# The down-projection of a retention and SwiGLU kernel as seven block products a group, with a new order of work

## The chip, the cores and the metric

The kernel runs on one core of a Trainium2 chip. The core has a matrix engine (TensorE, "PE" in the profile; its weight loads are shown as "PEld"), a vector engine (DVE), a scalar engine (ACT), GpSimd (POOL), and a queue that issues transfers (SyncE, "SP"). POOL also issues transfers. Each engine works through its own instructions in program order and waits on semaphores for the others. The metric is the device time of one execution in microseconds, and less is better.

## The reference

Two layers follow each other. The first is a recurrent retention over 768 positions, for 4 batches and 8 heads of 64 numbers; the second is a feed-forward layer with a gate:

```python
for t in range(S):
    state = gamma * state + einsum('bhd,bhe->bhde', k[:, :, t], v[:, :, t])
    y[:, :, t] = scale * einsum('bhd,bhde->bhe', q[:, :, t], state)
x  = y transposed to (3072 tokens, 512)
xn = x / sqrt(mean(x * x) + 1e-6) * rms_g
g  = xn @ w_gate                      # 512 x 1536
out = (g * sigmoid(g) * (xn @ w_val)) @ w_out      # 1536 x 512, float32 out
```

The last product, hidden values times `w_out`, is the down-projection.

## The kernel before

The 768 positions are cut into six chunks of 128. A *group* c is chunk c of all four batches b, 512 tokens. The state is not updated position by position: within a chunk the outputs come from masked scores, and the state is added once a chunk.

A group passes through these steps, each an operation with a short name:

- `Lq`, `Lk`, `Lv` (L304-316) load q, k, v of one chunk. Issued by POOL they are cast to bf16 on the way; issued by SP they arrive in f32 and `Cq`, `Ck`, `V` (L333-358) scale or cast them. For group 0, POOL's q and k loads come in a packed form ("q8", "k8", L310-312), which needs another way of transposing. Loads of group 2 wait for the last piece of `w_out` (L315-316).
- `Tq`/`Tk` with `Eq`/`Ek` transpose q and k on TensorE and copy the result out (groups 0 and 1); `tq`/`tk` (L387) do it by a transfer on SP's queue (groups 2 to 5). The packed form takes 16 small matmuls with the matrix `pick` (L364-367), the plain form four with `ident` (L371). `J` (L506) transposes the packed k back.
- `A` (L395) makes the scores of one or two batches, `M0`, `M1` (L421) mask them on DVE, `Y` (L432) multiplies them with v and adds the part from the state. `P` (L407) is a form of A for batches 2 and 3 of group 4 that starts the state's part early.
- `S` (ACT), `R` (POOL), `N` (DVE) are the normalization, `X` with `XE`, or `XE` on SP alone, the transposing of its result to `xnT`.
- `K` (L521) makes a chunk's addition to the state, four matmuls of 128x128x128 for the pairs of heads, of which only the blocks on the diagonal are used; `U` (L530) adds it to `st_f` on DVE, and `B` (L537, POOL) copies the state to bf16 for the next chunk.
- `g` and `v` (`ffn`, L544) are the two products of the feed-forward layer, four matmuls of 512 columns for each of 12 hidden tiles; `s` (ACT) and `h` (DVE) make the hidden values `hT`.
- `d` (L570) is the down-projection: for each batch 12 matmuls of 512 columns, accumulated over the hidden tiles in one PSUM bank; `o` copies the bank to SBUF, `st` stores it. The very last batch is cut into three pieces of columns (`e`, L593).
- `wg`, `wv`, `wo` load pieces of the weights through POOL's queue. `H` and `hot` are matmuls without use that keep TensorE busy in the first microseconds while data is on its way.

The order of all this is a list written out by hand or by a planner ahead of time, the string `ORDER` (L17-100): `g.2.5.6.0.4/5` is the operation g for group 2, hidden tiles 5 to 6, batches 0 to 4, in PSUM bank 5, and `@D`, `@A`, `@P`, `@S` choose the engine (DVE, ACT, POOL, SP). The loop at L600-604 issues the operations in that order, so each engine's own order is the list's. The eight PSUM banks are shared: an operation that takes a bank waits until the one before has been read out.

Of the kernel before, what the change touches and what calls it, by code (L numbers as in the profile page):

```python
# [9 lines left out]
F32 = mybir.dt.float32  # L10
# [7 lines left out]
H.8/3 yt Lk.0.2@S ident Ck.0.2@D vd Lk.1.1@S iota Tk.0.2/0 rms.1@S D.0.2@D Lk.0.0@P Lq.0.1@P H.3/1 Tk.0.0/2  # L18
H.1/1 Tq.0.1/7 Ek.0.0@D mk1 hot.3/1 J.0.0/3 D.0.0@D mk0 Lq.0.0@P Lk.0.1@P Tq.0.0/6 Lq.0.2@P Eq.0.1@A Eq.0.0@A
Tk.0.1/5 Ek.0.1@A Ek.0.2@D yd Lk.0.3@P H.1/1 Tq.0.2/4 tab Lq.0.3@P Eq.0.2@D hot.2/0 A.0.0/5017 M0.0.0 G/2 M1.0.0  # L20
Tq.0.3/6 Lv.0.0@P M0.0.1 GE@A Tk.0.3/3 Eq.0.3@A Lv.0.1@P M1.0.1 Lv.0.2@P Lv.0.3@P wg.0.2 Y.0.0/4 wv.0.2 A.0.2/21
wg.2.4 M1.0.2 Ek.0.3@A Lq.1.1@P H.3/0 A.0.3/61 S.0.0 M0.0.2 H.1/0 Y.0.2/3 K.0.0/0 J.0.1/5 M1.0.3 R.0.0 S.0.2
N.0.0 M0.0.3 Y.0.1/1 H.1/2 X.0.0/4 J.0.3/7 wv.2.4 S.0.1 XE.0.0@D U.0.0@A R.0.2 R.0.1 Ck.1.1@A N.0.2 B.0.0 H.2/2
Y.0.3/0 g.0.0.2.0.1/2 K.0.2/6 S.0.3 s.0.0.2.0.1 N.0.1 U.0.2@A wg.4.6 X.0.2/4 R.0.3 XE.0.2@D D.0.1@D
v.0.0.2.0.1/3 X.0.1/2 wv.4.6 causal XE.0.1@A Lk.1.2@P v.0.0.2.2.3/4 wg.6.9 Lq.1.2@P wv.6.9 h.0.0.2.0.1
g.0.0.2.2.3/6 D.0.3@D Lq.1.0@P g.0.0.2.1.2/5 g.0.2.3.0.3/3 s.0.0.2.2.3 h.0.0.2.2.3 s.0.0.2.1.2 g.0.3.4.0.3/6
N.0.3 v.0.0.2.1.2/4 D.1.1@D Tq.1.1/5 Lk.1.0@P Tk.1.1/0 X.0.3/7 Eq.1.1@D K.0.1/2 wg.9.12 v.0.3.4.0.3/1 Lv.1.1@P
s.0.3.4.0.3 XE.0.3@A g.0.0.4.3.4/6 s.0.2.3.0.3 h.0.0.2.1.2 g.0.4.6.3.4/4 wv.9.12 g.0.4.5.0.3/7 v.0.4.6.3.4/5
v.0.2.3.0.3/3 U.0.1@D s.0.4.6.3.4 Ek.1.1@A h.0.3.4.0.3 g.0.5.6.0.3/0 s.0.4.5.0.3 h.0.4.6.3.4 mc.0@P mc.1@P
v.0.4.5.0.3/5 v.0.0.4.3.4/7 h.0.2.3.0.3 Tk.1.2/1 g.0.6.7.0.4/4 Ek.1.2@A Lv.1.2@P h.0.4.5.0.3 g.0.7.8.0.4/2  # L30
Lv.1.0@P wo.0.4 Tq.1.2/1 s.0.5.6.0.3 s.0.7.8.0.4 Eq.1.2@D B.0.1 g.0.8.9.0.4/3 A.1.2/51 v.0.5.6.0.3/0 M1.1.2
wo.4.8 wo.8.12 s.0.0.4.3.4 v.0.7.8.0.4/2 h.0.0.4.3.4 h.0.5.6.0.3 h.0.7.8.0.4 Lk.1.3@P D.1.2@P Lk.2.0@S
v.0.6.7.0.4/7 Tk.1.0/0 M0.1.2 Lk.2.3@S Tq.1.0/6 v.0.8.9.0.4/1 s.0.6.7.0.4 Ek.1.0@A Eq.1.0@D h.0.6.7.0.4
s.0.8.9.0.4 Lq.2.1@S A.1.0/6042 M0.1.1 M1.1.0 B.0.2 M1.1.1 g.0.11.12.0.4/3 g.0.9.10.0.4/5 g.0.10.11.0.4/4
s.0.11.12.0.4 K.1.1/3 Y.1.1/0 s.0.10.11.0.4 h.0.8.9.0.4 S.1.1 U.1.1@D M0.1.0 v.0.9.10.0.4/2 v.0.10.11.0.4/3
R.1.1 v.0.11.12.0.4/4 s.0.9.10.0.4 K.0.3/7 h.0.9.10.0.4 D.1.0@P U.0.3@A Y.1.2/2 S.1.2 h.0.10.11.0.4 Y.1.0/3
N.1.1 h.0.11.12.0.4 Lq.1.3@P S.1.0 B.0.3 Lq.2.0@S Lk.2.1@S K.1.0/7 X.1.1/5 R.1.2 K.1.2/1 U.1.2@D d.0.3.0.4/0
N.1.2 R.1.0 N.1.0 d.0.0.0.4/6 XE.1.1@D d.0.1.0.4/4 d.0.2.0.4/2 X.1.0/5 d.0.3.4.8 X.1.2/1 d.0.0.4.8 Lv.1.3@P
d.0.1.4.8 XE.1.2@D d.0.1.8.12 U.1.0@D XE.1.0@A B.1.1 g.1.0.1.0.3/7 Tk.1.3/5 g.1.1.2.0.3/3 d.0.3.8.12 Tq.1.3/1
o.0.1@D Eq.1.3@D d.0.0.8.12 s.1.1.2.0.3 Ek.1.3@A o.0.3@A A.1.3/13 M1.1.3 Ck.2.0@A M0.1.3 tk.2.0 v.1.1.2.0.3/0  # L40
d.0.2.4.8 o.0.0@A Y.1.3/3 h.1.1.2.0.3 v.1.0.1.0.3/6 Ck.2.3@D S.1.3 R.1.3 Cq.2.1@D g.1.3.4.0.3/1 v.1.2.3.0.3/4
# [36 lines left out]
v.3.11.12.0.4/7 h.3.11.12.0.4 K.4.1/4 Lv.5.1@S Y.4.2.2 S.4.1 Y.4.3.2 S.4.2 V.5.1@P d.3.1.0.10/6 tk.5.3 tk.5.2
N.4.0 R.4.1 tk.5.1 st.2.0@S d.3.1.10.12 S.4.3 tq.5.3 N.4.1 R.4.3 o.3.1@A R.4.2 d.3.0.0.10/1 B.4.3 N.4.3 Lq.5.1@S
# [24 lines left out]
def kernel(  # L104
# [11 lines left out]
    nc = tc.nc  # L116
# [31 lines left out]
    def flat(x):  # L148
        return x.rearrange("p h d -> p (h d)")
# [485 lines left out]
```

## Time and profile before

| | |
|---|---|
| median of 3 runs | 233.62 us (233.48 to 234.39) |
| span of the profiled execution | 233.6 us (the page has no other time for it) |
| PE busy | 227.6 us |
| DVE, ACT, POOL busy | 130.4, 96.1, 89.7 us |
| mean granted clock of TensorE | 0.993 |
| moved by transfers | 33.61 MB, of which 25.70 MB by the hardware queue |
| read from and written to HBM | 28.31 MB, 6.29 MB |

Times in the traces count from the first instruction of the span. "Busy" matmul time overlaps from one matmul to the next, so the spacing of matmuls in the chain or the timeline is a better price than their mean duration. A bracket behind a row tells how long the engine had been idle before it, and what ended that.

### The profile page before, as it was taken

The numbers are of one execution on the slowest core, as the hardware profiler recorded it, in microseconds if no ns is written. First come the engines' busy times: TensorE is split into PE (matmuls) and PEld (weight loads), VectorE is DVE, ScalarE is ACT, GpSimd is POOL, SyncE is SP. The second block draws the span as 40 slices with busy tenths as digits, with TensorE's granted clock in tenths as the row PEclk, the third lists the DMA queues.
The fourth block names the chain that finished last, engine by engine and source line by source line (L and its number), as shares of the span: only waits on it lengthen the run. The fifth ranks groups of instructions, "written<-read, shape, count | busy, mean of one in ns | idle before, by whom it ended". The sixth has DMA issues, their size and how long they took to land.

```text
span 233.6 us, 4637 instructions
## 1 busy us (share of the span) xinstructions
PE 227.6 (97%) x1771; PEld 120.8 (52%) x1771; DVE 130.4 (56%) x241; ACT 96.1 (41%) x231; POOL 89.7 (38%) x163
## 2 busy tenths in 40 slices
PE   8799999999999999999999999999999999999994
PEld 2458855645545655445554444554455444444444
DVE  6479639753662965628975239866367532323320
ACT  7658433514337231464731346553265332232202
POOL 8958998550544555030273741247003100000000
PEclk9979999999999999999999999999999999999999
DMA  7999999999798888999988899968511400020222
GB/s 126 147 180 123 127 179 184 205 145 215 133 206 214 171 194 140 262 218 221 235 173 146 179 221 206 198 149 142 148 61 27 112 0 0 3 90 9 83 89 93
DMA packets 105353, 33.61 MB, mean 144 GB/s; under 512 B 94449, under 2 KB 102385, under 8 KB 105330
## 3 DMA queue, kind: packets, MB, share of 16 engines
q1 hardware_dynamic: 81858, 25.70, 50.2%
q0 software_dynamic: 23472, 7.60, 30.1%
q8 instruction: 14, 0.23, 0.4%
q14 instruction: 9, 0.07, 0.1%
HBM read 28.31 MB, written 6.29 MB: 148 GB/s over the span
## 4 chain that ended last, share of the span: by engine, by line
PE 89%; DMA 4%; POOL 2%; ACT 2%; DVE 1%; issue 0%; SPq 0%; POOLq 0%; DVEq 0%; ACTq 0%
PE v_ps L549 27%; PE g_ps L549 27%; PE o_ps L574 21%; PE a_ps L403 3%; DMA kb<-in_k_dram 3%; PE y_ps L441 2%; PE kv_ps L526 2%; PE y_ps L445 2%; DMA out_dram<-o_sb 1%; PE o_ps L596 1%; PE hot_ps L240 1%; PE t_ps L366 1%; PE t_ps L371 1%; PE xt_ps L495 1%; ACT xsq L455 1%; ACT xsq L458 1%
## 5 line engine op out<-in xcount | busy, mean ns | idle before, releaser
L567 DVE TENSOR_TENSOR hT<-sg,v_ps 128x512 bf16<-128x512 bf16 (+2 forms) x76 | 48.7, 656 | 47.8 <-PE v_ps L549 34.8
L549 PE MATMUL v_ps<-xnT,wv_b 128*128 128x512 bf16 (+2 forms) x344 | 71.2, 345 | 0.1
L559 ACT ACTIVATE sg<-g_ps 128x512 bf16<-128x512 f32 (+2 forms) x76 | 42.1, 575 | 70.6 <-PE g_ps L549 68.1
L549 PE MATMUL g_ps<-xnT,wg_b 128*128 128x512 bf16 (+2 forms) x344 | 70.0, 344 | 0.0
L574 PE MATMUL o_ps<-wo_b,hT 128*128 128x512 bf16 x276 | 63.5, 379 | 0.0
L549 PEld LDWEIGHTS <-wg_b 128*128 128x128 bf16 x344 | 30.4, 98 | 29.3
L549 PEld LDWEIGHTS <-wv_b 128*128 128x128 bf16 x344 | 30.2, 98 | 28.9 <-DVE am L426 0.6
L574 PEld LDWEIGHTS <-hT 128*128 128x128 bf16 x276 | 26.3, 98 | 29.1
L468 POOL TENSOR_SCALAR ms<-ssq 128x1 f32<-128x1 f32 x24 | 4.6, 190 | 59.1 <-ACT xsq L458 58.4
L426 DVE TENSOR_TENSOR am<-a_ps,causal 128x512 bf16<-128x512 f32 x32 | 20.6, 685 | 7.8 <-PE a_ps L403 7.5
L339 POOL TENSOR_TENSOR qb<-qf,ydec 128x512 bf16<-128x512 f32 x13 | 14.0, 1074 | 25.2 <-DMA qf<-in_q_dram 24.9
L146 ACT COPY o_sb<-o_ps 128x512 f32<-128x512 f32 (+1 forms) x16 | 8.8, 552 | 29.7 <-PE o_ps L574 23.1
L458 ACT ACTIVATE xsq<-y_ps 128x512 f32<-128x512 f32 x22 | 13.2, 599 | 18.9 <-PE y_ps L445 13.7
L482 DVE SCALAR_TENSOR_TENSOR xn<-y_ps,rstd,g_bc 128x512 bf16<-128x512 f32 x22 | 16.3, 748 | 4.3 <-POOL rstd L470 3.0
L146 DVE COPY o_sb<-o_ps 128x512 f32<-128x512 f32 (+1 forms) x10 | 6.4, 648 | 18.1 <-PE o_ps L574 12.2
L541 POOL CAST st_b<-st_f 64x256 bf16<-64x256 f32 x40 | 15.9, 398 | 1.3
L470 POOL TENSOR_TENSOR rstd<-ms,mhalf 128x1 f32<-128x1 f32 x24 | 13.3, 552 | 2.0
L534 DVE TENSOR_TENSOR st_f<-st_f,kv_ps 128x512 f32<-128x512 f32 x16 | 10.8, 684 | 5.2 <-PE kv_ps L526 4.6
L356 ACT ACTIVATE vp<-vf,vdec 128x64 bf16<-128x64 f32 x48 | 12.2, 343 | 0.0
L426 DVE TENSOR_TENSOR am<-a_ps,mask 128x512 bf16<-128x512 f32 x16 | 10.4, 686 | 2.5 <-PE a_ps L403 2.3
L240 PE MATMUL hot_ps<-one 128*128 128x512 bf16 x20 | 8.5, 547 | 1.1 <-DVE one L153 1.1
L441 PEld LDWEIGHTS <-am 128*128 128x128 bf16 x176 | 7.8, 99 | 3.1 <-issue 0.3
(99 smaller groups left out, 174.8 us busy)
## 6 DMA issues: line engine op xcount, KB each, us to landing
out_dram<-o_sb SPq DMA_DIRECT2D x23, 256.0 KB, 2.4
kf<-in_k_dram SPq DMA_DIRECT2D x18, 256.0 KB, 3.8
qf<-in_q_dram SPq DMA_DIRECT2D x16, 256.0 KB, 3.9
vf<-in_v_dram SPq DMA_DIRECT2D x16, 256.0 KB, 3.9
wo_b<-in_moe_w_out_dram POOLq DMA_DIRECT2D x3, 512.0 KB, 12.2
qb<-in_q_dram POOLq DMA_DIRECT2D x8, 128.0 KB, 6.6
vp<-in_v_dram POOLq DMA_DIRECT2D x8, 128.0 KB, 6.5
kb<-in_k_dram POOLq DMA_DIRECT2D x6, 128.0 KB, 5.9
```

The lines of the kernel that those rows point to most:

```text
L146: (e.copy if e is ACT else e.tensor_copy)(out, in_)
L339: e.tensor_tensor(out=u["qb"], in0=u["qf"], in1=ydec[:, c, :, None].to_broadcast([128, H, D]), op=ALU.mult)
L426: DVE.tensor_tensor(out=u["am"][:, i], in0=u["a"][i], in1=m, op=ALU.mult)
L441: nc.tensor.matmul(y[:, h, :], u["am"][:, h % 2, h // 2, :], u["vp"][:, h, :], start=h == 0, stop=c == 0 and h == H - 1, skip_group_check= ...
L458: ACT.activation(xsq, flat(u["y"]), AF.Square, accum_out=u["ssq"])
L470: POOL.tensor_tensor(out=u["rstd"], in0=ms, in1=mhalf, op=ALU.pow)
L482: DVE.scalar_tensor_tensor(out=u["xn"], in0=flat(u["y"]), scalar=u["rstd"], in1=g_bc, op0=ALU.mult, op1=ALU.mult)
L541: POOL.tensor_copy(st_b[b][r, :, i * 64:i * 64 + 64], st_f[b][r, :, i * 64:i * 64 + 64])
L549: nc.tensor.matmul(p[:, (n - n0) * m:(n - n0 + 1) * m], W[w][0][:, s, n * 128:(n + 1) * 128], xnT[c][:, s, b0 * C:b1 * C], start=s == 0, s ...
L559: ACT.activation(sg[:, :cols], done["wg", c, n0, b0][:, :cols], AF.Silu)
L567: DVE.tensor_tensor(out=hT[c][:, n0:n1, b0 * C:b1 * C], in0=sg, in1=p, op=ALU.mult)
L574: nc.tensor.matmul(o_ps[c, b], hT[c][:, n, b * C:(b + 1) * C], wo_b[:, n, :], start=n == 0, stop=n == NFF - 1)
```

## The change

**The down-projection.** The operations `d`, `o`, `st` and `e` are no longer used. The hidden values of a group are cut in two halves of tokens (batches 0 and 1, batches 2 and 3) and, within each block r of four hidden tiles, in two halves of tiles; `w_out` is cut in two halves of rows in the same way and in two halves of columns. The four quarters of the output are put together from seven products instead of eight:

- four sums of weights, once: w1 to w4 (each 1536 elements a partition, bf16);
- for each group and each of its three blocks r four sums of hidden quarters, z1 to z4 (each 512 elements a partition, bf16), on DVE or POOL; z3 takes the place of the quarter that it is made from;
- the products a1, a6, a7, a4 (in one bank, one on top of the other), b2, and c5, c3 (in one bank). One product is 12 matmuls of 256 columns: 2 halves of 128 tokens, 3 blocks r, 2 tiles each;
- between them the copies q1, q6, q7 of the bank a to SBUF, and the results r1 = b2 + q1, r2 = c5 + q7, r3 = c5 + c3 + q6 on DVE, and r4, a copy of the whole of a. s1 to s4 store the four quarters, 256 KB each.

**The state products** `K` become eight matmuls a chunk, one for each head, 64 columns wide and written to 64 partitions; `st_f` has half as many elements and `U` with it.

**Memory.** The masks share their buffers with the weight sums, two early tiles share the output buffers, `kd` and the z sums share twelve buffers, `hT` is kept in blocks of four tiles.

**The order** is new throughout. All eight q and k loads of group 0 are now in the packed form; four loads of group 1 stand ahead of the first weights; there are 12 matmuls of the kind H, not 20; the products of group 0 come in the middle of group 1's feed-forward work and those of group 3 in group 4's and 5's; the stores of results are spread out, and one of group 0 comes at the end.

The diff, cut to its core:

```diff
 ORDER = """
...
+hot.2/0 hot.3/1 Lq.0.1@P rms.1@S H.3/2 Lk.0.1@P Lq.0.3@P iota G/3 Lk.0.3@P Lk.0.0@P H.1/4 H.1/5 ident Lq.0.0@P
+Lq.0.2@P pick mk1 Lk.0.2@P vd H.1/6 Lv.0.3@P Tq.0.1/7 GE@D yt Lv.0.1@P mk0 Lv.0.0@P H.2/1 H.1/0 Eq.0.1@D Tq.0.3/2
+Tk.0.1/4 Ek.0.1@D Eq.0.3@A Tk.0.3/3 Tk.0.0/5 causal Ek.0.3@D Lv.0.2@P Tq.0.0/6 J.0.1/7 D.0.1@D A.0.3/10 M0.0.3
+Ek.0.0@A J.0.0/2 D.0.0@D Eq.0.0@A A.0.0/4356 J.0.3/7 Lk.1.3@P Lk.1.2@P M1.0.3 Y.0.3/1 S.0.3 Lk.4.2@S Lk.1.1@S yd
+Lq.1.2@P Tk.0.2/2 Lq.1.3@P Ck.1.1@A Ek.0.2@A M1.0.0 M0.0.0 K.0.0/0 Tq.0.2/3 Eq.0.2@A U.0.0@A D.0.3@D wg.2.4 wg.0.2
...
+v.0.6.7.0.4/0 h.0.6.7.0.4 g.1.6.7.0.4/6 s.0.8.9.0.4 g.1.1.2.0.3/2 v.0.7.8.0.4/3 Ck.2.2@P Lv.2.0@S s.1.2.3.0.3
...
+v.1.7.8.0.4/5 h.1.7.8.0.4 a1.0.0.3/1 A.2.2/2743 q1.0@D M0.2.3 B.1.1 g.1.11.12.0.4/6 tq.2.0 Lk.3.2@S s.1.11.12.0.4
...
+s.3.10.11.0.4 Lq.5.1@S Cq.5.1@P P.4.2/125406 M1.4.3 g.3.2.3.0.4/3 g.3.5.6.0.4/7 s.3.5.6.0.4 M0.4.3 M1.4.2 M0.4.2
...
+a4.5.2.3.0 r4.5.0@D c3.5.2.3.1 c3.5.2.3.0 a4.4.0.3 s4.5.0@S r3.5.1 r3.5.0 s3.5.0@S s3.5.1@S r4.4@A s4.4@S
...
-        u["kv"] = bank(bk[0], [128, NHP, 128], F32, "kv_ps")
-        for hp in range(NHP):
-            nc.tensor.matmul(u["kv"][:, hp, :], flat(k)[:, hp * 128:(hp + 1) * 128],
-                             u["vp"][:, 2 * hp:2 * hp + 2, :], start=True, stop=True)
+        u["kv"] = bank(bk[0], [128, NHP, D], F32, "kv_ps")
+        for h in range(H):
+            nc.tensor.matmul(u["kv"][h % 2 * D:h % 2 * D + D, h // 2, :], k[:, h], u["vp"][:, h, :],
+                             start=True, stop=True)
...
+    def quarter(c, r, i, j):
+        return hT[c, r][:, (J0, J1)[j], (LO, HI)[i]]
...
+    def zsum(i, e, c, r, x, a, b, how):
+        if x is None:
+            x = sb.tile([128, 2, GT // 2], BF16, name="z", tag="kd", bufs=KD)
+        e.tensor_tensor(out=x, in0=a, in1=b, op=how)
+        done["z", i, c, r] = x
...
+    def product(x, i, bk, c, r0, r1, p=None):
+        first = i in (1, 2, 5) and r0 == 0
+        if first:
+            done[x, c] = bank(bk[0], [128, 2, HM], F32, x)
+        for q in (0, 1) if p is None else (p,):
+            for r in range(r0, r1):
+                for k in (0, 1):
+                    nc.tensor.matmul(done[x, c][:, q], left(i, c, r)[:, k, q * C:q * C + C], right(i)[:, r, k],
+                                     start=first and q == r == k == 0, stop=r == 2 and k == 1, skip_group_check=True)
...
+    def keep(i, e, c):
+        done["q", i, c] = ring([128, 2, HM], F32, "sn", SN)
+        copy(e, done["q", i, c], done["a", c])
...
+    QUARTER = {1: ("b", 1, 0, 0), 2: ("c", 7, 1, 1), 3: ("c", 6, 0, 1), 4: ("a", None, 1, 0)}
...
+            DVE.tensor_tensor(out=done["r", i, c][:, s], in0=done[x, c][:, s], in1=done["q", q, c][:, s], op=ALU.add)
```

259 lines of the change are left out of this document (149 added, 110 removed).

## The prediction

> **What bounds the kernel now.** I read the page's busy shares and slices first, then the chain of work that ended last, then the groups by form and the engines' timelines.
>
> ```profile
> span 233.6 us, 4637 instructions
> ...
> PE 227.6 (97%) x1771; PEld 120.8 (52%) x1771; DVE 130.4 (56%) x241; ACT 96.1 (41%) x231; POOL 89.7 (38%) x163
> ...
>
> DMA  7999999999798888999988899968511400020222
> ...
> PE 89%; DMA 4%; POOL 2%; ACT 2%; DVE 1%; issue 0%; SPq 0%; POOLq 0%; DVEq 0%; ACTq 0%
> ```
>
> TensorE is busy from end to end and 89% of the last chain; no other engine passes 56%. But the DMA line stands mostly at 8 or 9 for the first 29 slices (170 us): the transfers are nearly as full as TensorE. A gain on TensorE counts only if the inputs come earlier too. The end, from the chain in order of time:
>
> ```profile
> 220.04 7.77 PE o_ps L574 x36
> 227.81 2.66 PE o_ps L596 x36
> 230.47 0.02 issue
> 230.50 0.32 ACT o_sb L146
> ```
>
> The last matmul ends at 230.47; a copy and a store take the other 3.13 us. All sums below are against the profiled span of 233.6, which is also the median of the runs (233.62).
>
> **The change part by part.** *The down-projection.* The group row counts what goes:
>
> ```profile
> L574 PE MATMUL o_ps<-wo_b,hT 128*128 128x512 bf16 x276 | 63.5, 379 | 0.0
> ...
> L596 PEld LDWEIGHTS <-hT 128*128 128x128 bf16 x36 | 2.7, 98 | 0.2
> ```
>
> Mean durations overlap (379 ns), so the price is the spacing in the chain: 7.77/36 = 215.8 ns for 512 columns, 0.4215 ns a column. The 36 matmuls of L596 (24 of 192 columns, 12 of 128: 6144) take 2.66, 0.433 ns a column. Before: 276 x 0.2158 + 2.66 = 62.2 us. After: 6 groups x 7 products x 12 matmuls = 504 of 256 columns. That width is not in the trace; between 0.4215 and 0.433 ns a column it costs 107.9 to 110.8 ns. I take the middle, 109.3: 55.1 us. **Saved: 7.1 us** (6.4 to 7.8). The 216 extra weight loads are free as long as a 98 ns load hides under its neighbour's 109 ns; at L596 loads of 98 ns already hide under matmuls spaced 74 ns.
>
> The Trainium skill, "TensorE: Matmul & The Clock Gate", section "Back-to-back issue gap", speaks against this: it gives a sustained spacing of 131 ns at 512 columns and 81 at 128, so half a width would cost far more than half. An estimate from that page is 98 ns at 256 columns, 49 us after against 38 before, and the sum would come out slower; the chain's 215.8 ns contradicts its 512-column figure, which leaves it the small chance below.
>
> *State products* (K, 20 of them): four 128-column matmuls become eight of 64 columns on 64-row outputs. The same shape stands in the early transposes (L366). From TensorE's timeline:
>
> ```profile
> 1.11 3.60 PE L240 MATMUL hot_ps<-one 128*128 128x512 bf16 x8 [1.11 <-DVE one L153]
> ...
> 7.42 0.44 PE L366 MATMUL t_ps<-pick,qb 128*64 128x64 bf16 x16
> 7.80 0.34 PE L234 MATMUL hot_ps<-one 128*128 128x128 bf16 x3
> ...
> 41.34 0.39 PE L526 MATMUL kv_ps<-vp,kd 128*128 128x128 bf16 x4
> 41.56 0.40 PE L441 MATMUL y_ps<-vp,am 128*128 128x64 bf16 x8
> ```
>
> Sixteen take 0.38 us start to start, so eight take 0.19, against 0.22 now: 20 x 0.03 = **0.6 us saved**. Against that, b = 2 of group 0 now comes in the packed form too: one more re-transpose J (0.22, as four of 128 columns) and 0.38 instead of 0.22 for its T: **0.4 lost**. TensorE's net: 7.1 + 0.6 - 0.4 = 7.3 us.
>
> *Sums and copies.* 72 z (512 bf16 elements a partition; 44 on DVE, 28 on POOL), 4 w (three times that), 18 q copies, and additions in place of 18 of the 24 output copies. No row shows bf16 + bf16 from SBUF; the neighbours:
>
> ```profile
> L146 DVE CAST kb<-kf 128x512 bf16<-128x512 f32 x8 | 3.3, 418 | 0.0
> ...
> L517 DVE TENSOR_TENSOR kd<-kb,vdec 128x512 bf16<-128x512 bf16 x3 | 2.1, 686 | 0.3 <-ACT vdec L259 0.3
> ...
> L517 POOL TENSOR_TENSOR kd<-kb,vdec 128x512 bf16<-128x512 bf16 x2 | 2.1, 1035 | 0.1
> ...
> L146 ACT COPY o_sb<-o_ps 128x512 f32<-128x512 f32 x14 | 8.2, 586 | 28.0 <-PE o_ps L574 23.1 <-DMA out_dram<-o_sb 4.8
> ```
>
> A z on DVE lies between 0.42 and 0.69; I take 0.42, as both its inputs are 16 bits wide and kd has an f32 one. DVE then goes from 130 to about 163 us (z 18, w 2, additions and copies 19 more, other moved work 4, less the old copies and the halved state additions, 11); at 0.69, 177. POOL: 28 x 1.04 + two w of 3.1 = 35, less 3 moved away: about 122. ACT falls to 88. All stay under the span, so I cost them at nothing on the path: TensorE's g and v of other groups cover them. Locally it is tight. In the stretch of 20 us of matmul work that ends at the first product, DVE has 15 us to do at 0.42 and 19 at 0.69; only the second would hold up banks, by 1 or 2 us. A slowed z delays h and state copies queued behind it on DVE, and those hold PSUM banks.
>
> DVE and POOL also meet. Around 125 us:
>
> ```profile
> 125.31 0.68 DVE L358 TENSOR_TENSOR vp<-vf,vdec 128x512 bf16<-128x512 f32 x1
> ...
> 125.52 1.37 POOL L339 TENSOR_TENSOR qb<-qf,ydec 128x512 bf16<-128x512 f32 x1 [2.22 <-DMA qf<-in_q_dram]
> ...
> 129.75 1.04 POOL L339 TENSOR_TENSOR qb<-qf,ydec 128x512 bf16<-128x512 f32 x1 [2.85 <-DMA qf<-in_q_dram]
> ```
>
> The same POOL instruction took 1.37 beside a DVE one that reads two SBUF tensors and 1.04 alone; DVE paid nothing (0.68). So each z on DVE can delay POOL by up to 0.33 us: at most 44 x 0.33 = 15 us on an engine with 100 us to spare, but POOL's q scalings stand behind it. The Trainium skill, "GPSIMD Engine Reference", section "Key points", says that the two share their SBUF interfaces, with contention when DVE has two SBUF inputs; these rows agree.
>
> *The start.* POOL issues the loads and the weights in order:
>
> ```profile
> 6.17 3.59 POOL L314 DMA_DIRECT2D vp<-in_v_dram  x4
> ...
> 9.99 0.76 POOL L323 DMA_DIRECT2D wg_b<-in_moe_w_gate_dram  x1 [0.23 <-DMA kb<-in_k_dram]
> ...
> DMA to landing us min/median/max: 4.9/7.2/10.7
> ```
>
> The last row is wv_b's. Four group-1 loads (0.9 each) and one more group-0 load now stand ahead of the weights, so the first wg issue moves from 10.0 to about 15 and wv.4.6 to about 26.4, behind four R and both mc. First g: about 22.8 instead of 19.4, but by then all of group 0's and much of group 1's attention is done; the useful matmul work done by 22.8 is equal, 9.9 us. wv.4.6 lands at 31 to 34 (26.4 + 4.9 to 7.2); the old kernel has as much done by 31.3 as the new one at that point. So the start costs 0 to 2: **+1.0**. The fillers H drop from 20 to 12 (8 x 0.45, by the first row of the fence on TensorE, or x 0.22 at full clock: 1.7 to 3.6 us), but they only filled waits for data, so I count nothing; if data came no later, that would be gain. PEclk falls to 7 in the third slice even with them; a second such slice would cost 0.3 x 5.8 = 1.7 us, inside these bounds.
>
> *The middle.* Group 2's loads wait for the last piece of wo, and so does w1 on POOL, with group 2's q scalings (Cq) queued behind its 3.1 us:
>
> ```profile
> 50.77 1.01 SPq L314 DMA_DIRECT2D kf<-in_k_dram  x2
> ...
> 149.35 0.62 PE L403 MATMUL a_ps<-qT,kT 64*128 64x128 bf16 x16
> ...
> 165.58 0.55 PEld L549 LDWEIGHTS <-wv_b 128*128 128x128 bf16 x4 [0.61 <-DVE am L426]
> ...
> L387 SPq DMA_TRANSPOSE kT<-kb x16: 1195/1222/1681, 57.5 to 162.4; - x16
> ...
> L314 SPq DMA_DIRECT2D qf<-in_q_dram x16: 572/580/1457, 51.8 to 153.2; - x16
> ```
>
> wo should land about 0.7 later, at 51.5. w1 to 54.6, Cq's to 57.7, transposes behind them: the first scores of group 2 can start at about 66.5, and TensorE comes to them at about 68. Then the decisive stretch, up to P.4.2 (149.35 in the fence). The new order has 17.5 us less useful work ahead of it (three down-projections of 10.4 become two of 9.2, four g or v of 0.86 and one pair of scores move behind it), so TensorE asks at about 133. Until then SP must issue 43 loads, 35 transposes and 3 stores: 46 x 0.58 + 35 x 1.22 = 69 us in 81.5, possible. They move 46 x 0.262 + 35 x 0.131 = 16.6 MB, 204 GB/s. The windows give:
>
> ```profile
> 60.00:80.00 20.00, 20.00 (x151) 10.98 (x150) 11.18 (x19) 10.02 (x25) 9.91 (x16) 1.00 0.89 197
> 80.00:100.00 20.00, 20.00 (x159) 10.31 (x157) 12.83 (x22) 5.91 (x13) 8.03 (x16) 1.00 0.93 189
> 100.00:120.00 20.00, 20.00 (x158) 10.60 (x157) 14.44 (x23) 12.05 (x34) 5.93 (x13) 1.00 1.01 226
> 120.00:140.00 20.00, 20.00 (x103) 9.16 (x103) 8.69 (x14) 5.05 (x10) 11.38 (x18) 1.00 0.86 172
> ```
>
> At 226 nothing is late; at the mean of 196 it is 85 us, 3.4 late; at 172, 15 late. Old rates were partly demand, so I lean to the high side: waits of 1.5 us in place of the old kernel's 1.0 (0.61 in the fence and 0.4 near 159), **+0.5**. Thirteen old stores before the last scores of group 5 become seven; the others return at the end, 3.4 MB in the last 19 us (179 GB/s), under these rates.
>
> *The end.* From the page's DMA issues:
>
> ```profile
> out_dram<-o_sb SPq DMA_DIRECT2D x23, 256.0 KB, 2.4
> ...
> out_dram<-o_sb SPq DMA_DIRECT2D x2, 96.0 KB, 1.7
> ```
>
> The last copy is 512 wide, 0.59 instead of 0.32, and its store 256 KB instead of 96: 0.27 + 0.7 = **+1.0**.
>
> Sum: 233.6 - 7.3 + 1.0 + 0.5 + 1.0 = **228.8 us**, 2.1% faster.
>
> **The rivals.** *A, the forecast:* 225.5 to 231. *B, no waits at all:* fillers gone at full clock, no late weights, no middle waits: 228.8 - 1.0 - 1.5 - 1.7 = 224.6. For it: the order puts products, which need only SBUF data, where inputs are late; against: the POOL queue above. *C, the other side: the inputs of groups 3 and 4 come too late,* the mechanism of the middle. At 172 GB/s it adds 14: 243. It decides below 189 GB/s (16.6 MB in 81.5 + 6.3 us): slower than before. For it: the DMA line at 9, and a mean of 186 over the old stretch (45 loads, 32 transposes, 9 stores: 18.3 MB in 98.6 us); against: 226 held for 20 us. *D, DVE and POOL become the bound:* z at 0.69 and contention, 1 to 2 us at the first products, and as much at the last z: 230.5 to 232.5. *E, weight loads not hidden:* 216 x 98 ns = 21 us more, 250; the row of L596 speaks against it. The Trainium skill's spacing ("TensorE: Matmul & The Clock Gate") would end in this case.
>
> **How the numbers follow.** A 0.52, B 0.14, C 0.24 (of which 0.16 slower, 0.08 within), D 0.08 (0.06 faster), E 0.02. So faster 0.72, same 0.10, slower 0.18; half a per cent (1.2 us) is about what a measurement of this kernel can tell from no change. Range: 224.0 (B) to 235.5 (C, not far past its point of decision).
>
> **What would show it.** Products spaced at 109 ns; first g near 23; TensorE's idle before P.4.2 and A.5 under 2 us; z on DVE at 0.42; the last matmul near 224.7 and 4 us behind it. Wrong if TensorE shows waits for kT, qT or xnT of groups 3 to 5 of over 5 us, if products are spaced over 125 ns, or if waits for wv reach past 35 us.

## The result, and the profile after

The changed kernel takes 235.87 us (median of 4, 235.18 to 236.45) beside 233.8 for the kernel before: a ratio of 1.0084, 95% interval 1.0056 to 1.0112. It is slower by 2.07 us, 0.8%, where 4.8 less was forecast. Medians and ratios here and below leave out executions over 1.5% above the fastest of their kernel. From the page of the profiled execution (236.33 us, span 234.5):

```profile
span 234.5 us, 5291 instructions
...
PE 223.9 (95%) x2051; PEld 140.2 (60%) x2051; DVE 164.9 (70%) x311; ACT 91.7 (39%) x212; POOL 129.7 (55%) x192
...
PEclk9985999999999999999999999999999999999999
DMA  6999999999799979999979986894700700120263
...
PE 71%; DMA 8%; DVE 6%; POOL 4%; SPq 2%; issue 2%; ACT 1%; ACTq 0%; POOLq 0%; DVEq 0%
```

The busy times are nearly those forecast (DVE 164.9 for 163, ACT 91.7 for 88, POOL 129.7 for 122), and TensorE works less. But its share of the last chain fell from 89% to 71%: transfers, DVE and POOL now stand in it with 18%. The chain also has the products and the last one, start and length:

```profile
79.38 1.31 PE c L656 x12
...
229.27 1.32 PE a L656 x12
```

1.31/12 = 109.2 ns a product's matmul, as forecast (109.3). The last matmul ends at 230.6 and 3.9 us lie behind it. TensorE's waits, in total, times and the longest:

```profile
PE y_ps L452 <- DVE am L437: 2.2, 5, 1.0
PE hot_ps L242 <- DVE one L161: 1.1, 1, 1.1
PE g_ps L560 <- DVE hT L582: 1.1, 2, 0.6
PE kv_ps L537 <- DVE kd L528: 0.6, 1, 0.6
PE a_ps L414 <- DMA qT<-qb: 0.6, 2, 0.3
PE y_ps L452 <- DVE vp L369: 0.5, 1, 0.5
PE a L656 <- ACT r L148: 0.5, 1, 0.5
```

The kernel before has only the second of these and 1.4 us for a first key load. Nearly all new waits are for DVE, and each is short. To see what they sum to, I laid each operation's start beside the matmul work in front of it, priced by its spacing. After 36 us the changed kernel falls back by 0.80, 0.63 and 0.41 us between 70 and 77, by 0.65 at 99, by 0.42, 0.63 and 0.32 between 137 and 149 and by 0.62 at the very end: 4.5 us. The kernel before loses 1.0 there.

The first of them shows how it comes about. DVE and POOL just ahead of 77 us:

```profile
70.49 0.77 DVE L350 TENSOR_TENSOR qb<-qf,ydec 128x512 bf16<-128x512 f32 x1 [2.10 <-DMA qf<-in_q_dram]
71.19 1.27 DVE L582 TENSOR_TENSOR hT<-sg,v_ps 128x512 bf16<-128x512 bf16 x2
...
74.18 1.69 DVE L369 TENSOR_TENSOR vp<-vf,vdec 128x512 bf16<-128x512 f32 x1
```

```profile
72.24 3.08 POOL L614 TENSOR_TENSOR w<-wo_b,w 128x1536 bf16<-128x1536 bf16 x1
```

DVE, the fullest engine of this stretch, stood 2.1 us for a query load with two hidden values queued behind; then a v scaling that costs 0.68 elsewhere took 1.69 beside POOL's weight sum. Forms of DVE after:

```profile
L369 DVE TENSOR_TENSOR vp<-vf,vdec 128x512 bf16<-128x512 f32 x7 | 6.2, 883 | 0.3 <-DMA vf<-in_v_dram 0.3
L629 DVE TENSOR_TENSOR z<-hT 128x512 bf16<-128x512 bf16 x14 | 5.9, 419 | 0.1
L629 DVE TENSOR_TENSOR z<-z,hT 128x512 bf16<-128x512 bf16 x11 | 5.6, 506 | 0.3 <-POOL z L629 0.2
...
L629 DVE TENSOR_TENSOR hT<-hT 128x512 bf16<-128x512 bf16 x9 | 5.4, 605 | 0.1
L350 DVE TENSOR_TENSOR qb<-qf,ydec 128x512 bf16<-128x512 f32 x4 | 4.0, 993 | 2.1 <-DMA qf<-in_q_dram 2.1
```

A z costs 0.42 alone, as forecast, but up to 0.61 in the mean of a group, and a query scaling 0.99 where the forecast's neighbours had 0.69.

### The profile page after: what moved, and what is told of

Same layout as the page of the kernel before. It is cut to its first block, busy times and chain, and to the rows that moved or that the text cites. A ratio compares the mean times of both kernels' runs of the same rounds, so it can differ in the third digit from the quotient of the medians.

```text
span 234.5 us, 5291 instructions
## 1 busy us (share of the span) xinstructions
PE 223.9 (95%) x2051; PEld 140.2 (60%) x2051; DVE 164.9 (70%) x311; ACT 91.7 (39%) x212; POOL 129.7 (55%) x192
## 4 chain that ended last, share of the span: by engine, by line
PE 71%; DMA 8%; DVE 6%; POOL 4%; SPq 2%; issue 2%; ACT 1%; ACTq 0%; POOLq 0%; DVEq 0%
PE g_ps L560 23%; PE v_ps L560 22%; PE a L656 10%; PE c L656 6%; DMA qf<-in_q_dram 5%; DVE am L437 3%; PE y_ps L452 2%; POOL qb L350 2%; PE b L656 2%; DMA kf<-in_k_dram 2%; PE y_ps L456 2%; PE a_ps L414 2%; SPq L398 2%; PE kv_ps L537 1%; DVE hT L582 1%
## 5 line engine op out<-in xcount | busy, mean ns | idle before, releaser
L560 PE MATMUL g_ps<-xnT,wg_b 128*128 128x512 bf16 (+2 forms) x344 | 71.0, 345 | 1.1 <-DVE hT L582 1.1
L656 PEld LDWEIGHTS <-hT 128*128 128x128 bf16 x288 | 27.8, 98 | 5.8 <-issue 0.6
L656 PEld LDWEIGHTS <-z 128*128 128x128 bf16 x216 | 20.9, 98 | 3.3
L469 ACT ACTIVATE xsq<-y_ps 128x512 bf16<-128x512 f32 x22 | 13.2, 598 | 19.7 <-PE y_ps L456 16.3
L552 POOL CAST st_b<-st_f 64x256 bf16<-64x256 f32 x40 | 17.2, 430 | 6.1 <-PE y_ps L456 2.8
L656 PE MATMUL a<-wo_b,hT 128*128 128x256 bf16 x144 | 17.9, 273 | 0.1
L629 POOL TENSOR_TENSOR z<-hT 128x512 bf16<-128x512 bf16 x4 | 4.8, 1198 | 22.2 <-DVE hT L582 22.2
L629 POOL TENSOR_TENSOR hT<-hT 128x512 bf16<-128x512 bf16 x9 | 11.7, 1308 | 2.5 <-DVE z L629 2.3
L452 PE MATMUL y_ps<-vp,am 128*128 128x64 bf16 x176 | 9.6, 198 | 2.7 <-DVE am L437 2.2
L148 ACT COPY sn<-a 128x512 f32<-128x512 f32 x11 | 6.4, 586 | 13.2 <-PE a L656 13.1
```

The lines of the kernel that those rows point to most:

```text
L452: nc.tensor.matmul(y[:, h, :], u["am"][:, h % 2, h // 2, :], u["vp"][:, h, :], start=h == 0, stop=c == 0 and h == H - 1, skip_group_check= ...
L469: ACT.activation(xsq, flat(u["y"]), AF.Square, accum_out=u["ssq"])
L552: POOL.tensor_copy(st_b[b][r, :, i * 64:i * 64 + 64], st_f[b][r])
L560: nc.tensor.matmul(p[:, (n - n0) * m:(n - n0 + 1) * m], W[w][0][:, s, n * 128:(n + 1) * 128], xnT[c][:, s, b0 * C:b1 * C], start=s == 0, s ...
L629: e.tensor_tensor(out=x, in0=a, in1=b, op=how)
L656: nc.tensor.matmul(done[x, c][:, q], left(i, c, r)[:, k, q * C:q * C + C], right(i)[:, r, k], start=first and q == r == k == 0, stop=r == ...
```

## The experiments

The forecast had TensorE's gain at 7.3 us. Theories for its loss: **T1**, the 64-column state products cost instead of saving; **T2**, the z and w sums, through DVE and POOL, make TensorE wait; **T3**, the rival C of the prediction, the transfers' rate makes inputs late; **T4**, the start. Ratios below are to the kernel before, run on the same chip, with 95% intervals. The runs were made on different chips, where the medians of the kernel before lie between 233.8 and 234.2 us, so a difference of a few tenths to the changed kernel says nothing.

### The state products

The three rows in which K stands in the changed kernel, and the same place of a run of the kernel before with K alone changed:

```profile
40.37 1.03 PE L560 MATMUL g_ps<-xnT,wg_b 128*128 128x512 bf16 x4
41.33 0.32 PE L537 MATMUL kv_ps<-vp,kd 128*64 128x64 bf16 x8
41.58 0.41 PE L452 MATMUL y_ps<-vp,am 128*128 128x64 bf16 x8
```

```profile
43.85 0.39 PE L445 MATMUL y_ps<-st_b,qT 128*128 128x128 bf16 x4
44.16 0.32 PE L526 MATMUL kv_ps<-vp,kd 128*64 128x64 bf16 x8
44.41 0.40 PE L495 MATMUL xt_ps<-ident,xn 128*128 128x128 bf16 x4
```

Four matmuls of 512 columns from 40.37 end at 40.37 + 4 x 0.2158 = 41.23; K starts at 41.33, and what follows starts 0.25 after that. A K that stands alone costs 0.34 us of TensorE's time (14 of the changed kernel after 24 us and 16 of the other), where the old form cost 0.22. Two stand side by side:

```profile
118.76 1.15 PE L656 MATMUL a<-w,hT 128*128 128x256 bf16 x9
119.84 0.44 PE L537 MATMUL kv_ps<-vp,kb 128*64 128x64 bf16 x16
120.21 1.48 PE L656 MATMUL c<-w,z 128*128 128x256 bf16 x12
```

The pair takes 0.37 from its start, and its second K starts 0.147 behind the first. So eight matmuls take 0.147, and a stay in the 64-column form costs 0.09 to enter and 0.08 to 0.10 to leave. The Trainium skill, "TensorEngine Tiling (Array Packing)", section "Key Properties", says that a change of tiling mode drains TensorE; these rows agree and give the price. T1: 20 x 0.115 = 2.3 us lost if every K stands alone, not 0.6 saved. In the changed kernel 18 do, and 16 in the run with K alone changed; the others are pairs, 0.47 us where the old form takes 0.45. That makes 2.1 and 1.9 us.

**e2_k_new_before**, the kernel before with this edit alone:

```diff
-            nc.tensor.matmul(u["kv"][:, hp, :], flat(k)[:, hp * 128:(hp + 1) * 128],
-                             u["vp"][:, 2 * hp:2 * hp + 2, :], start=True, stop=True)
+            nc.tensor.matmul(u["kv"][h % 2 * D:h % 2 * D + D, h // 2, :], k[:, h], u["vp"][:, h, :],
+                             start=True, stop=True)
```

> The kernel before with the state products alone changed to the 64-column form. T1: 20 times 0.115 us more, about 236.1 us, ratio near 1.010. The prediction's term: 0.6 us less, about 233.2 us, ratio 0.997.

Measured: 235.49, ratio 1.0063 [1.0040, 1.0086], about +1.5 us. The sign is T1's and the prediction's is refuted; the 1.9 us of the rows lie inside the interval.

**e1_k_old**, the reverse edit in the changed kernel (`kd` and z share eleven buffers and three small tiles share others to make room):

> The changed kernel with the state products as they were before the change: four 128-column matmuls per K and a state of full width on VectorE. Theory T1 (each K pays for entering and leaving the 64-column form, 20 times about 0.115 us more than the old K): about 2.3 us less than the changed kernel, 233.6 us, ratio to before near 0.999. The prediction's own term (the 64-column form saves 0.6 us): about 0.6 us more than the changed kernel, 236.5 us. The wider state on VectorE adds 20 times 0.27 us = 5.4 us of work there, which would take back up to 1 us if VectorE is what TensorE waits for.

Measured: 236.07, ratio 1.0099 [1.0059, 1.0139]: nothing came back, a miss for T1. The old form needs the wide state on DVE (0.68 us a sum for 0.41, 16 of them). So the new form costs TensorE and spares DVE, and in the changed kernel the two may come out even. That DVE took the gain, and not the shared buffers, was argued and not tried, so T1's price is shown in time for the kernel before alone.

### The sums

**e3_no_sums**, **e6_no_pool_sums** and **e7_no_dve_sums** leave sums out: all, those of POOL, those of DVE. The edit (for e6; e3 and e7 likewise), and the same for `wsum` with a plain quarter of `w_out`:

```diff
     def zsum(i, e, c, r, x, a, b, how):
+        if e is POOL:
+            done["z", i, c, r] = wg_b[:, 0:2, 0:256]
+            return
```

> The changed kernel with all sums for the seven products left out: the z sums and the w sums are not formed, and the products take a resident weight slice and plain quarters of w_out in their place, so the output is not the reference's; TensorE's work and all transfers stay. Theory T2 (VectorE and GpSimd, loaded and slowing each other, cause the waits in the middle): 2.0 to 3.5 us less than the changed kernel, 232.4 to 233.9 us, and TensorE's waits at A.2, P.4 and A.4 gone. Rival T3 (the transfers' rate alone makes the inputs late): within 0.5 us of the changed kernel.

> The changed kernel without the sums that GpSimd forms (28 of the z sums and two weight sums; what uses them takes a resident weight slice or a plain quarter of w_out, so the output is not the reference's); VectorE's own sums stay. T2a (GpSimd's queue and its slowing of VectorE): most of the 2.25 us that leaving out all sums gave comes back here, 234.1 us or less. T2b (VectorE's own load): under 0.7 us of it, 235.2 us or more.

> The changed kernel without the sums that VectorE forms (44 of the z sums and two weight sums, replaced in the same way, so the output is not the reference's); GpSimd's sums stay. T2a: under 0.7 us less than the changed kernel, 235.2 us or more. T2b: most of the 2.25 us, 234.1 us or less.

Measured: e3 233.62, 0.9993 [0.9967, 1.0019]; e6 234.17, 1.0018 [0.9986, 1.0049]; e7 235.97, 1.0092 [1.0057, 1.0126]. Against the changed kernel the sums cost 2.2 us in all, POOL's alone 1.7, DVE's nothing. A part of this may be the clock of the first 24 us, where these edits change nothing: three of the changed kernel's four executions have a mean granted clock of 0.984 to 0.985, but two of e3's ten and four of e6's ten have one of 0.982 to 0.985. Among these alone the means are 236.06, 234.41 and 235.29, so 1.7 us for all sums and 0.8 for POOL's. T2 holds, in the form that POOL's sums do it, at 0.8 to 1.7 us. How they reach DVE is in e6's page:

```profile
PE 222.1 (95%) x2026; PEld 140.1 (60%) x2051; DVE 159.2 (68%) x311; ACT 91.6 (39%) x212; POOL 90.6 (39%) x162
```

DVE does the same 311 instructions in 159.2 us, not 164.9: POOL's sums cost DVE 5.7 us by slowing it.

**e5_w_dve** and **e9_all_dve** move sums instead:

```diff
-X.1.2/6 z2.0.0@P w1@P v.0.11.12.0.4/5 Cq.2.3@P X.1.1/4
+X.1.2/6 z2.0.0@P w1@D v.0.11.12.0.4/5 Cq.2.3@P X.1.1/4
...
-A.2.0/3052 S.2.3 Lv.3.3@S V.3.3@A z4.0.1@P w4@P
+A.2.0/3052 S.2.3 Lv.3.3@S V.3.3@A z4.0.1@P w4@D
```

(e9: every z and w on DVE, w1 just ahead of w2.)

> The changed kernel with the two weight sums that GpSimd forms (3.09 us each there) formed by VectorE (0.95 us each) at the same places of the order. Theory T2a (the waits at 70 to 77 us, 1.84 us in all, come from VectorE's work being late because GpSimd is full and slows it): 1.0 to 1.8 us less than the changed kernel, 234.1 to 234.9 us. Theory T2b (VectorE's own load is the cause): VectorE has 1.9 us more to do in front of those waits, so the same time or up to 1 us more, 235.9 to 236.9 us.

> The changed kernel with every sum on VectorE: the 28 z sums of GpSimd at 0.42 us each there in place of 1.2, and its two weight sums, just ahead of their readers. VectorE gets 13.7 us more to do, GpSimd 40 us less. If GpSimd's sums are what costs (by its queue or by slowing VectorE): 234.2 to 235.0 us. If VectorE's own load decides: 235.9 us or more. The long VectorE forms (over 1.3 us for a product scaling or a z sum) should be gone from its trace if they come from GpSimd's two-input work beside them.

Measured: e5 238.77, 1.0228 [1.0191, 1.0265]; e9 236.02, 1.0094 [1.0059, 1.0130]. e5 was a badly placed step and tells neither theory apart:

```profile
49.64 0.96 DVE L530 TENSOR_TENSOR w<-wo_b 128x1536 bf16<-128x1536 bf16 x1 [3.74 <-DMA wo_b<-in_moe_w_out_dram]
```

On POOL w1 waited for the weights where little stood behind it; on DVE everything did. e9 missed the gain and teaches more; its number is that of the other branch, VectorE's own load. The slowing is nearly gone (rows of its DVE):

```profile
L545 DVE TENSOR_TENSOR hT<-hT 128x512 bf16<-128x512 bf16 x18 | 8.1, 453 | 0.1
...
L545 DVE TENSOR_TENSOR z<-hT 128x512 bf16<-128x512 bf16 x18 | 7.5, 419 | 0.2
```

and the waits at 70 to 77 us with it, yet the time is not. DVE at 99 us, in e9 and then in the changed kernel:

```profile
98.83 0.43 DVE L64 CAST kb<-kf 128x512 bf16<-128x512 f32 x1 [2.91 <-DMA kf<-in_k_dram]
99.17 0.68 DVE L498 TENSOR_TENSOR hT<-sg,v_ps 128x512 bf16<-128x512 bf16 x1
```

```profile
99.15 0.75 DVE L148 CAST kb<-kf 128x512 bf16<-128x512 f32 x1 [1.50 <-DMA kf<-in_k_dram]
99.81 0.67 DVE L582 TENSOR_TENSOR hT<-sg,v_ps 128x512 bf16<-128x512 bf16 x1
```

TensorE comes 1.6 us earlier, but the key load is issued at 95.3 in both kernels and lands when it did; DVE stands longer for it, with the hidden value that TensorE needs queued behind.

### Late inputs

**e13_no_stores** takes 3 MB from the transfers:

```diff
-s4.0@S
-s1.0@S
...
-s3.2@S
```

> The changed kernel without the twelve stores of groups 0 to 2 (their output stays unwritten, so the output is not the reference's): 3 MB less for the DMA engines, which are 94 to 98% busy from 60 to 150 us. If their rate holds the inputs back in the middle (the rival on record as late inputs): the waits at 138 and 143 us for the transposed queries and at 99 us behind a late key load shrink, 0.7 to 1.5 us less, 234.4 to 235.2 us. If not: within 0.4 us of the changed kernel.

Measured: 235.45, 1.0064 [1.0043, 1.0085], 0.4 less than the changed kernel: at the edge, and not the 0.7 that T3 asks. The interval holds 0.7 less as well as no change: the transfers' rate is not shown to matter, and a small share of it is not ruled out.

**e16_inputs** leaves the transfers as they are and takes late inputs out of the way of other work (on top of e9, with the fillers of e4, the end of e8, and one z sum of group 4 earlier):

```diff
-tq.3.2 Lk.3.0@S Ck.3.0@D v.2.0.1.0.4/2
+tq.3.2 Lk.3.0@S v.2.0.1.0.4/2
...
-M0.3.2 tq.3.0 M1.3.2
+M0.3.2 tq.3.0 M1.3.2 Ck.3.0@D
...
-Cq.4.3@P tq.4.3 tq.5.3 Ck.4.3@P
+Cq.4.3@P tq.4.3 Ck.4.3@P tk.4.3 tq.4.2
```

> The changed kernel with every sum on VectorE, the six early fillers and the end without its wait for the copy, and the order mended where the run with all sums on VectorE still waits: VectorE's key cast of group 3 (it stood 2.9 us there for a load issued at 95 us, with hidden values queued behind) moved behind the next masks; the two transposes that the scores of group 4 wait for put ahead of three of group 5 on SyncE; one z sum of group 4 earlier. If late inputs standing in the engines' queues are what took the place of the sums: 236.0 less 0.85, 0.45, 1.4, 1.0 and 0.8, so 231.5 to 233.0 us. If VectorE's load itself is the limit: 235 us or more.

Measured: 234.62, 1.0017 [0.9984, 1.0051]: 1.25 us less than the changed kernel (1.6 by the ratios), not the 3 hoped for, and level with the kernel before. In its profile TensorE's waits for qT, for hidden values and for the copy at the end are gone:

```profile
PE y_ps L368 <- DVE am L353: 2.1, 4, 1.2
PE hot_ps L158 <- DVE one L77: 1.1, 1, 1.1
PE hot_ps L164 <- DVE kd L444: 0.5, 1, 0.5
PE xt_ps L422 <- DVE xn L409: 0.2, 1, 0.2
```

Against e9 this is 1.4 us less, and the fillers alone measured 0.85 (below). So that the place of a waiting instruction in an engine's queue held TensorE is read from the rows at 70 and 99 us; e16 agrees, but what its moves gave without the fillers and the end was not tried.

### The start

**e4_fillers** adds seven throw-away matmuls (three, two and two) among TensorE's early waits:

```diff
-Y.0.3/1 S.0.3
+H.3/2 Y.0.3/1 S.0.3
...
-K.0.3/4 Y.0.0/7
+H.2/4 K.0.3/4 Y.0.0/7
...
-Y.0.1/2 R.0.3
+H.2/2 Y.0.1/2 R.0.3
```

> The changed kernel with six more of the throw-away matmul stretches in TensorE's early waits, as the kernel before had more of them. Theory T4 (the longer half-clock stretch at the start, 6.8 us against 3.4, costs 1.7 us): 1.0 to 1.7 us less, 234.2 to 234.9 us. Rival: the waits for the first inputs hide it, within 0.3 us of the changed kernel, or up to 0.5 us more where a filler runs past the input's arrival.

Measured: 235.02, 1.0045 [1.0016, 1.0074], 0.85 us less: between the two, and not clear of the changed kernel's interval. All ten of its executions have a mean granted clock of 0.996 or more; the one execution of the changed kernel with such a clock, 0.999, took 235.18. So the fillers may do no more than keep the clock up in every execution. The stretch from 12 to 24 us (PE busy, then the other engines, granted clock, DMA share, GB/s) in the kernel before, in e2 with the same order, in the changed kernel and in e4:

```profile
12.00:24.00 12.00, 11.95 (x173) 8.30 (x172) 10.55 (x19) 8.15 (x21) 8.22 (x17) 0.86 1.46 150
```

```profile
12.00:24.00 12.00, 12.00 (x212) 9.26 (x205) 11.25 (x21) 8.25 (x21) 10.07 (x19) 1.00 1.48 160
```

```profile
12.00:24.00 12.00, 9.56 (x157) 7.26 (x157) 10.32 (x19) 8.43 (x21) 11.35 (x19) 0.72 1.87 177
```

```profile
12.00:24.00 12.00, 10.13 (x179) 6.96 (x174) 10.43 (x19) 8.72 (x21) 11.35 (x19) 1.00 1.88 179
```

The changed kernel is idle for 2.4 of these 12 us and at 0.72 of the clock. With the fillers the clock is back at 1.00, but 1.9 us of idle time stay. What ended TensorE's waits in the changed kernel was DVE:

```profile
13.34 0.38 PE L452 MATMUL y_ps<-vp,am 128*128 128x64 bf16 x7 [0.99 <-DVE am L437]
...
15.13 0.32 PE L537 MATMUL kv_ps<-vp,kd 128*64 128x64 bf16 x8 [0.58 <-DVE kd L528]
...
16.33 0.61 PE L452 MATMUL y_ps<-vp,am 128*128 128x64 bf16 x8 [0.54 <-DVE am L437]
```

DVE itself works from 9.34 to 16.3 us with one gap of 0.17, and had stood 1.47 before that for a transposed key. Whether later loads or the order of DVE's steps cost the start its time was not tried.

Matmul work other than fillers that stands behind TensorE at 36.3 us: 25.6 us in e2, 22.1 in the changed kernel, 22.5 in e4. The first g comes at 23.70 (forecast 22.8). The start costs 3.5 us against an execution whose clock was not cut, or 3.1 with the fillers; the one that the prediction read had its own stretch at 0.50 to 0.70 (23.9 us of work by then).

### Versions to beat both

**e8_best** (e4, with w1 and w4 on DVE ahead of their readers, Cq.2.1 on POOL, and at the end c3 between the copy r4 and the product that waits for it; the last is the cure of the end that e10, e16 and e17 have too):

```diff
-a4.5.2.3.1 r4.5.1@A r3.4 s3.4@S s4.5.1@S a4.5.2.3.0 r4.5.0@D c3.5.2.3.1 c3.5.2.3.0
+a4.5.2.3.1 r4.5.1@A r3.4 s3.4@S s4.5.1@S c3.5.2.3.1 c3.5.2.3.0 a4.5.2.3.0 r4.5.0@D
```

**e11_pairs_alone** sets state products side by side, **e10_pairs** does it on top of e9 with the cures of e4 and of the end, **e17_inputs_pairs** on top of e16, with one weight sum and one z sum moved behind a mask. One of the pairs:

```diff
-K.2.1/2 b2.0.0.3/6 a4.0.0.3
+b2.0.0.3/6 a4.0.0.3
...
-K.2.3/7 r2.0
+K.2.1/2 K.2.3/7 r2.0
```

> The changed kernel with the cures put together: the six early fillers (0.85 us measured alone), the two weight sums of GpSimd on VectorE just ahead of their readers, group 2's last query scaling on GpSimd with its load issued earlier in place of VectorE (which stood 2.1 us for that load), and at the end two of group 5's products put between the copy and the matmul that waited 0.46 us for it. If the waits add up as the theories say: 0.85 + 1.2 + 0.45 = 2.5 us less, 233.4 us, ratio to before near 0.998. If VectorE's load takes the place of the wait that goes: 234.5 us.

> The changed kernel with five state products moved to stand right beside another (three of chunk 1 in a row, two pairs of chunk 2 and 3, three in a row at chunks 3 and 4), so that TensorE enters and leaves the 64-column form 5 times less. T1 (0.092 us to enter and 0.10 to leave, 0.147 us for the product itself): about 1.0 us less in TensorE's time, 234.9 us if no wait takes it up. Rival (the extra 0.115 us lies in each product's weight loads, not in entering and leaving): no change.

> All cures together: every sum on VectorE, the state products side by side, the six early fillers, and the end without its wait for the copy. If they add up: 235.9 less 1.2, 1.0, 0.85 and 0.45, so 232.4 us, ratio to before 0.993. If VectorE, with 179 us to do, becomes what TensorE waits for: 234 us or more.

> As e16_inputs, with two more steps: one weight sum and one z sum on VectorE moved behind the group 2 mask that TensorE waited 1.2 us for, and five state products put right beside another, as in e11_pairs_alone, where waits for inputs hid what that gave. T1 (0.19 us to enter and leave the 64-column form): with the waits out of the way 5 times 0.2 us = 1.0 us shows, and the mask gives up to 1.2: 232.4 to 233.6 us, ratio to before 0.993 to 0.998. If other waits take its place again: 234.6 us.

Measured: e8 235.01, 1.0051 [1.0027, 1.0076]; e11 236.50, 1.0094 [1.0060, 1.0127]; e10 236.19, 1.0084 [1.0056, 1.0112]; e17 235.03, 1.0044 [1.0021, 1.0067]. Only the fillers' 0.85 shows in e8. Side by side the state products do take less of TensorE (three in a row 0.50 us from the first to what follows, by e11's timeline: 43.54 to 44.04), but no time came of it in e11, e10 or e17. e11's profile has waits that the changed kernel's has not, 0.8 us of them for state sums on DVE; that these took it was not tried. e17's executions lie between 233.4 and 236.0, and its profile is of the second fastest; it is no evidence for the median.

**e12_groups34**, **e14_groups34b** and **e15_group4** go the other way: the kernel before, order, K and end included, with the products in groups 3 and 4 alone, or in 4 alone, all sums on DVE:

```diff
-d.4.0.0.10/6 d.4.1.0.10/5 v.5.1.2.0.4/2
+a1.4.0.3/6 q1.4@D b2.4.0.3/5 r1.4 a6.4.0.3 q6.4@A v.5.1.2.0.4/2
...
+z1.4.0@D z2.4.0@D z3.4.0@D z4.4.0@D
```

> The kernel before, with its order, its state products and its end, in which groups 3 and 4 alone get the seven products: their z sums (24, 0.42 us each) and the four weight sums (0.95 us each) all on VectorE, in the stretch after 135 us where VectorE was 35 to 60% busy, GpSimd had nothing two-input left and most loads were done. TensorE's gain is 2 times (48 times 215.8 ns less 84 times 109.2 ns) = 2.4 us. If the products' gain is real and only the sums beside a full middle, the state products and the end took it: 231.4 to 232.2 us, ratio 0.989 to 0.993. If the sums cost TensorE as much wherever they stand: 234 us or more.

> As e12_groups34 (the kernel before with the seven products in groups 3 and 4 alone), with the sums out of the way of the attention steps: the weight sums at 129 to 137 us, the state sum of group 4 ahead of the z sums it stood behind, the copy after product 7 on ScalarE and not in front of group 5's masks on VectorE, a z sum that is not needed at once behind those masks. Theory (the 10 us that e12_groups34 lost are VectorE's work standing in the wrong place of its queue, the products' gain of 2.4 us is there): 231.6 to 233.0 us. If the sums' load alone is enough to lose the gain in the stretch from 145 to 165 us: 234 us or more.

> The kernel before with the seven products in group 4 alone (195 to 219 us; its sums on VectorE from 181 to 195 us, the weight sums at 129 to 137 us). Gain on TensorE 1.2 us. Theory: 232.6 to 233.4 us, ratio 0.994 to 0.998. If sums cost TensorE wherever they stand: 234 us or more.

Measured: e12 243.83, 1.0421 [1.0395, 1.0446]; e14 237.40, 1.0135 [1.0094, 1.0176]; e15 233.34, 0.9989 [0.9965, 1.0014]. In e12 TensorE stands at two places:

```profile
162.21 0.79 PE L320 MATMUL a_ps<-qT,kT 64*128 64x128 bf16 x15 [2.50 <-DVE st_f L451]
...
170.53 1.04 PE L466 MATMUL v_ps<-xnT,wv_b 128*128 128x512 bf16 x4 [2.05 <-DVE am L343]
```

The first for a bank whose state sum stood behind z sums on DVE, the second for a mask behind a copy that itself stood 5.3 us for a product. e14, with these out of the way by other places in the queue and by one copy moved to ScalarE, is 6.4 us better, and still slower than before. Its profile shows why in the main, by TensorE's waits and the chain:

```profile
PE v_ps L466 <- DMA xnT<-xn: 2.0, 1, 2.0
```

```profile
164.19 2.15 PE a L573 x12
166.34 2.14 PE c L573 x12
```

TensorE waits 2.0 us for a transposed result of the normalization and 0.5 for a z sum, while DVE is busy without a break from 158 to 164 us. Two products behind these waits take 2.15 us each and not 1.31: the granted clock is 0.57 from 164 to 168 us, where the kernel before has 1.00. That is 4.2 us, of the 3.6 that e14 is above the kernel before and the 2.4 that did not come.

In group 4, where DVE has room, the products cost nothing; of their 1.2 us the ratio shows 0.3, with an interval from 0.8 less to 0.3 more. No version beat the kernel before beyond doubt.

## Why the prediction was wrong

Its terms beside what the runs and traces give, in us (the kernel before taken as an execution at full clock):

| step | forecast | found |
|---|---|---|
| down-projection and early transposes on TensorE | -6.7 | -6.8, by the work in the order at the measured spacings |
| state products | -0.6 | +1.5 (e2), 2.1 by their rows |
| start | +1.0 | +3.5 |
| middle | +0.5 | +2.9 (3.9 of waits, 1.0 before) |
| end | +1.0 | +1.4 (0.8 behind the last matmul, 0.6 for the bank) |
| sum | -4.8 | +2.5, with 1.5 for the state products; the medians say +2.07 |

e3 bears the table out: without any sum the changed kernel is level with the one before (0.9993), so the state products, the start and the end alone use up what the products save.

**Right:** the products' spacing, the price of a z alone, the engines' busy times, the hidden weight loads (rival E), the tail of 3.9 us. That 109.3 came so close is in part luck: it is the middle of two bounds, 107.9 and 110.8. The estimate of 98 ns from the Trainium skill ("TensorE: Matmul & The Clock Gate", section "Back-to-back issue gap") is not what the trace gives, 109.2. The 38 us before that the prediction worked out with it should be 39.

**The step "state products" failed, in sign.** It took sixteen matmuls of the early transposes, 0.38 us start to start, and halved them. But 16 x 18.4 ns are 0.29; the rest of that row is the leaving of the form, once a stay, and halving the row halved a fixed price. The entering stood in front of the row and was not seen. A stay of eight costs 0.34 us, not 0.19. Rows of one shape inside a long run do not show what a short stay costs.

**The step "sums and copies" failed where it says "All stay under the span, so I cost them at nothing on the path" and "DVE paid nothing".** One pair of rows, in which POOL paid, was read as a rule for who pays. After, DVE pays as well: z up to 1.37, v scaling 1.69 for 0.68, and 5.7 us over the whole kernel by e6. The Trainium skill, "SBUF — State Buffer", section "SBUF: two separate sides", says that the shared ports are held for a whole instruction by whichever of the two starts first and that the other waits; the 1.69 beside a POOL sum of 3.08 agrees. The v scaling ended 0.55 us behind that sum. Rival D had this mechanism, at 1 to 2 us; e3 puts the sums at 1.7 to 2.2.

**The step "the start" was mis-sized** by 2.5: the useful work by 22.8 us is not equal, but about 2 us less in the changed kernel. It was compared with an execution that had lost some 1.7 us to a low clock (25.6 less 23.9), and its PEclk row, a 7 in the third slice, said so. What made the rest of the start longer stays open.

**The base of the sum was not the median.** The prediction takes the span of 233.6 for the time of 233.62. In the executions on record the time is 1.7 to 2.1 us above the span, so the profiled one took about 235.4 us (an estimate from these), above the four that were timed beside the changed kernel, and the sum's 228.8, a span, would be about 230.6 as a time. That 233.6 and 233.62 agree was chance.

**The step "the middle"** had the right place but another mechanism: not the rate of 189 GB/s but, by the rows at 70 and 99 us, casts and scalings that wait for loads in DVE's queue, in front of hidden values. Its own test, over 5 us of waits for kT, qT or xnT of groups 3 to 5, did not fire: those waits are 0.6. It looked at TensorE's direct wait, while the lateness came through DVE.

Open stay 0.4 to 0.9 us between the terms and the profiles, what the start's 3.5 us are made of, what of the sums' cost is slowing and what is queueing (e9 takes both away and adds load), and about 1.8 us of e14.

## What to carry to other kernels

Price a short stay in another form of an engine by its entering and leaving, not by the spacing inside a long run of it. Before moving work to an engine with free time, look at how full it is in the stretch in question, and at what stands behind the moved step in its queue: 6 us hung on places in e12, and a share of 70% over the span hid a stretch of 15 us at 94%. And check the granted clock of the execution that a sum is made against, slice by slice.

## What the hardware showed

- Entering the form with 64-row outputs costs TensorE about 0.09 us and leaving it 0.08 to 0.10; inside it a matmul of 64 columns takes 18.4 ns.
- GpSimd's bf16 sums of 512 elements take 1.15 us where VectorE's take 0.42, and of 1536 elements 3.09 for 0.95; 39 us of them slowed VectorE by 5.7 us.
- Between the profiles of two executions, one with seven more throw-away matmuls of 512 columns in early waits, the granted clock from 12 to 24 us went from 0.72 to 1.00; all ten executions with them had a mean clock of 0.996 or more, and three of four without had 0.985 or less.
